# A linear-attention block with a gated feed-forward on one core: the query products regrouped around a burst of k^T v, and the gate and up weights loaded from the first query group on

## The chip, the cores and the metric

The kernel runs on one core of one Trainium2 chip. The metric is the device time of one execution in microseconds, the median of several runs. Of the kernel before there are three: 271.57, 271.64 and 271.98 us, median 271.64.

The core's engines run programs of their own and meet at semaphores: TensorE (PE in the profile, with its weight loads as PEld) multiplies matrices into PSUM, ScalarE (ACT) and VectorE (DVE) do elementwise work and read PSUM, GpSimd (POOL) does elementwise work on SBUF, and SyncE (SP) issues DMA transfers.

## What is computed

One sequence of S = 2048 rows with D = 640 columns. First a layer norm and linear attention with H = 32 heads of 20 columns, then a layer norm and a gated feed-forward of width F = 1536; each adds its input back.

```python
q, k, v = split_heads(layernorm(x) @ wqkv)
pq, pk = q @ w_phi[h], k @ w_phi[h]
phi_q = concat(softmax(pq), softmax(-pq)); phi_k = concat(softmax(pk), softmax(-pk))
kv = sum_s phi_k[s].T @ v[s];   z = sum_s phi_k[s]
o = (phi_q @ kv) / (phi_q @ z + 1e-6)
h = x + o @ wo
h2 = h + (gelu(layernorm(h) @ w_gate) * (layernorm(h) @ w_up)) @ w_down
```

## The kernel before

The rows are cut into 16 tiles of 128, four tiles make a block, and the 640 columns are cut into five chunks of 128. TensorE's and SyncE's order is written out by hand in the source, and within the kernel's main part that of the other engines too; each engine runs its instructions strictly in that order.

In the first part w_phi is folded into the weights of k and q, and a loop over the tiles (line 494) makes, for each tile, the key features (k_tile: ten products, two exponentials on ScalarE), the values (v_mm, v_ev) and the sums and factors that normalise the features (k_norm: VectorE sums, takes reciprocals, and GpSimd and VectorE multiply). kv_tile (line 368) adds a tile's phi_k^T v into the PSUM tile kvp with 32 small products a tile. It is called in bursts: tiles 0 to 3 at t = 9, 4 to 8 at t = 13, 9 to 12 at t = 15 (the third burst, table KVQ), and 13 to 15 after the loop (the last burst). Each burst needs the normalised features of its tiles.

The query features are made per block and chunk: product number 5 b + c is block b, chunk c. The table QG (line 52) groups them; a group of one or two such products, each five matmuls of 512 columns (one for each chunk of the inner dimension), has one PSUM tile of two banks and one SBUF tile Eq. q_mm(j) (line 387) issues the matmuls of group j, q_exp(j) (line 399) two exponentials on ScalarE over the whole group, one for each sign. The first four groups, (5, 6), (0, 1), (2, 3) and (4,), are made at t = 15 (table QT); the third burst stands behind the second group, (0, 1). The fifth group, (7, 8), follows the last burst, and its last matmul stands behind the first tile's attention (lines 831 to 835). Block 0 is chunks 0 to 4; block 1 is 5 to 9.

kv_mask (line 377) lets VectorE mask and transpose the finished kvp into KV; from then on attn_a (line 648) multiplies query features with KV, attn_b, attn_b2 and attn_b3 divide, the result o is transposed (for tile 0 by a DMA on SP's queue, for tile 1 on TensorE) and attn_c multiplies it with W_o. Behind that come the second layer norm, gate_up (line 758) and down (line 775), woven with the attention of later tiles.

The weights W_gate (tile Wg) and W_up (Wu) arrive by SP's queue. A GpSimd copy of one column from Eq into Wg (line 536) holds the first transfer of Wg back until group 2's second exponential, since the transfer writes what the copy wrote; two transfers of Wg's first four fifths follow at once (line 538). The rest of Wg and all of Wu are issued by load_up (line 551), which is called behind attn_b3(0), so that in SP's queue they stand behind the transpose of tile 0's o.

PSUM is handed out as four tiles of two banks each; a matmul that writes a tile waits until whoever read the tile earlier is done.

Of the kernel before, what the change touches and what calls it, by code (L numbers as in the profile page):

```python
# [11 lines left out]
ACTF = mybir.ActivationFunctionType  # L12
# [5 lines left out]
def kernel(  # L18
# [12 lines left out]
    nc = tc.nc  # L31
# [8 lines left out]
    NC = D // P  # L40
# [8 lines left out]
    LQ = (7, 8, 9, 9, 10)  # L49
    FQ = (10, 11, 12, 13, 14)  # L50

    QG = ((5, 6), (0, 1), (2, 3), (4,), (7, 8), (9, 10), (11, 12), (13, 14), (15,), (16,), (17,), (18,), (19,))
    QT = (15, 15, 15, 15)
    T3 = 3

# [32 lines left out]
    Wg = const.tile([P, NC, FF], BF16, name="Wg")  # L88
    Wu = const.tile([P, NC, FF], BF16, name="Wu")
# [5 lines left out]

    Eq = [const.tile([P, len(g), 2, 512], BF16, name=f"Eq{j}") for j, g in enumerate(QG)]
    ident = const.tile([P, P], BF16, name="ident")
# [5 lines left out]
    def eq(t, c, s):  # L103
        for E, g in zip(Eq, QG):
            if t // 4 * NC + c in g:
                return E[:, g.index(t // 4 * NC + c), s, t % 4 * P:(t % 4 + 1) * P]
# [4 lines left out]
    def gtile(name):  # L111
        return psG.tile([P, 2, 512], F32, name=name, tag="G")
# [46 lines left out]
    def transpose_to(dst, src, on_pe, on_dve=False):  # L159

        if on_pe:
            tp = psG.tile([P, 16, P], BF16, name="tp", tag="G")
            for c in range(NC):
                nc.tensor.transpose(tp[:, c, :], src[:, c * P:(c + 1) * P], ident)  # L164
            (nc.vector.tensor_copy if on_dve else nc.scalar.copy)(dst, tp[:, 0:NC, :])  # L165
        else:
            nc.sync.dma_start_transpose(dst, src)
# [32 lines left out]
    def load_T(WT, i, *ds):  # L200

        for d in ds:
            nc.sync.dma_start_transpose(WT[:, :, d * P:(d + 1) * P], A_wqkv[d * P:(d + 1) * P, i * D:(i + 1) * D])
# [3 lines left out]
    wg_v = B_w_gate.rearrange("(c p) n -> p c n", p=P)  # L207
    wu_v = B_w_up.rearrange("(c p) n -> p c n", p=P)
# [23 lines left out]
    def fold(WT, W2, quarters, ds=range(NC)):  # L232


        n, w = (2, QF) if quarters else (1, HD)
        runs = []
        for c in range(NC):
            lo, hi = H0[c] * Dh, (H0[c] + NH[c]) * Dh
            for r in range(2 * n):
                a, b = max(lo, r * w), min(hi, (r + 1) * w)  # L240
                if a < b:
                    runs.append((r // n, r, c, a, b))
        runs.sort()
        for d in ds:
            wa = gtile("wa")
            wr = wa.rearrange("p u (q x) -> p (u q) x", q=n)
            for i, (u, r, c, a, b) in enumerate(runs):
                nc.tensor.matmul(wr[:, r, a - r * w:b - r * w], lhsT=WT[:, c, d * P:(d + 1) * P],  # L248
                                 rhs=BD[:, c].rearrange("p a b -> p (a b)")[:, a - H0[c] * Dh:b - H0[c] * Dh],
                                 start=(i == 0 or runs[i - 1][0] != u),  # L250
                                 stop=(i + 1 == len(runs) or runs[i + 1][0] != u), skip_group_check=True)
            dst, src = W2[:, d, :].rearrange("p (u f) -> p u f", u=2), wr[:, :, 0:w]
            if quarters:
                dst = W2[:, d, :].rearrange("p (c r f) -> p r c f", c=NC, r=4)
                src = src.rearrange("p r (c f) -> p r c f", c=NC)
            if d in (QA if quarters else KA):
                nc.scalar.copy(dst, src)
            else:
                nc.vector.tensor_copy(dst, src)
# [15 lines left out]
    def ln_st(*tiles, act=True, between=None, log=False):  # L275
        for t, v in zip(tiles, ln_stats(p1, [x_sb[t // 4][:, t % 4, :] for t in tiles], "1", act, between, log)):
            lnp[t] = v

    def ln_ap(t, on_act=False, on_pe=False):
        ln = (ln_act if on_act else ln_dve)(p1, "1", *lnp[t])  # L280
        if on_pe:
            lnp[t] = ln
        else:
            transpose_to(LN1T[t // 4][:, :, t % 4 * P:(t % 4 + 1) * P], ln, False)
# [16 lines left out]
    def v_mm(t, us=(0, 1)):  # L301
        if 0 in us:
            pv[t] = gtile("pv")
        proj(pv[t], t, Wv, us)
# [10 lines left out]
    def v_ev(t):  # L315
        nc.scalar.activation(vS[t % NV][:, :, 1:VC].rearrange("p (u h) f -> p u h f", u=2),
                             pv[t][:, :, 0:HD].rearrange("p u (h f) -> p u h f", f=Dh), ACTF.Copy,
                             scale=lnp[t][2] if t in CT else 1.0)
# [12 lines left out]
    def k_tile(t):  # L331
        if t in pks:
            pk = pks[t]
            k_part(t, NC - 1)
        else:
            pk = gtile("pk")
            proj(pk, t, Wk2)
        Ek[t] = ev.tile([P, 2, D], BF16, name="E", bufs=10)
        for s in range(2):
            nc.scalar.activation(Ek[t][:, s, :].rearrange("p (u f) -> p u f", u=2), pk[:, :, 0:HD],  # L340
                                 ACTF.Exp, scale=((lnp[t][2], nrstd[t]) if t in CT else (1.0, -1.0))[s])
# [26 lines left out]
    def kv_tile(t):  # L368

        E = Ek[t].rearrange("p s (h f) -> p s h f", f=Dh)  # L370
        for i in range(QH):
            for r in range(4):
                h = r * QH + i
                nc.tensor.matmul(kvp[QUAD[r], :, i * Dh:(i + 1) * Dh], lhsT=vF[t % NV][:, h * VC:h * VC + 32],  # L374
                                 rhs=E[:, :, h, :], start=(i == t == 0), stop=(t == NT - 1), skip_group_check=True)
# [9 lines left out]
    pqs = {}  # L385

    def q_mm(j, part=(0, 1), kcs=range(NC)):

        if 0 in part and 0 in kcs:
            pqs[j] = gtile("pq")  # L390
        for i, bc in enumerate(QG[j]):
            if i not in part:
                continue
            b, c = divmod(bc, NC)
            for kc in kcs:
                nc.tensor.matmul(pqs[j][:, i, :], lhsT=Wq2[:, kc, c * P:(c + 1) * P], rhs=LN1T[b][:, kc, :],  # L396
                                 start=(kc == 0), stop=(kc == NC - 1))

    def q_exp(j, signs=(0, 1)):
        for s in signs:  # L400
            nc.scalar.activation(Eq[j][:, :, s, :], pqs[j][:, 0:len(QG[j])], ACTF.Exp, scale=(1.0, -1.0)[s])  # L401

    def st_act(t, i):

# [89 lines left out]
    for t in range(NT):  # L494
        if t == T3:
            kvp = gtile("kvp")[:, 0, 0:2 * QF].rearrange("p (s f) -> p s f", s=2)
        late = t in (1, 4)
        if 0 < t < NT - 6 and not late:
            ln_ap(t + 6, on_act=True)
        k_tile(t)  # L500
        if t == 0:
            ln_ap(6)
            nc.sync.dma_start(x_sb[3][:, 0:2, :], x_v[:, 12:14, :])
        if t in FQ:
            fold(WqT, Wq2, True, [i for i, f in enumerate(FQ) if f == t])
        for i in KVG.get(t, ()):
            kv_tile(i)
        for j in range(len(QT)):
            if t == QT[j]:
                q_mm(j)  # L510
                q_exp(j)
                for i in KVQ.get(j, ()):
                    kv_tile(i)
        if 0 < t < NT - 3:
            v_mm(t + 3)
        if late:
            ln_ap(t + 6, on_act=True)
        if t == 1:
            nc.sync.dma_start(x_sb[3][:, 2:4, :], x_v[:, 14:16, :])
        if 0 < t < NT - 3:  # L520
            v_ev(t + 3)
        for i in ST.get(t, ()):
            ln_st(i, i + 1)
        k_norm(t)
        load_T(WqT, 0, *[i for i, f in enumerate(LQ) if f == t])
        if t == 10:
            transpose_to(LN1T[0][:, :, P:2 * P], ln_a(1), False)
        if t == 13:
            ln_ap(0, on_act=True)
        if t == 8:  # L530
            for z in KT:
                nc.gpsimd.memset(z, 0.0)
        if t == 13:
            nc.sync.dma_start(Wo, wo_v)
    q = len(QT)
    nc.gpsimd.tensor_copy(Wg[:, 0, 0:1], Eq[q - 2][:, 0, 1, 0:1])
    for a, b in ((0, 2), (2, 4)):
        nc.sync.dma_start(Wg[:, a:b], wg_v[:, a:b])
    for t in range(13, NT):
        kv_tile(t)  # L540
    kv_mask()
# [5 lines left out]
    p2r = ctx.enter_context(tc.tile_pool(name="p2r", bufs=1, side="right", reuse_waits="tile"))  # L547
    Wd = p2r.tile([P, NF, D], BF16, name="Wd")
    wd_v = B_w_down.rearrange("(c p) n -> p c n", p=P)

    def load_up():

        nc.sync.dma_start(Wg[:, 4:NC], wg_v[:, 4:NC])
        nc.sync.dma_start(Wu, wu_v)

    def load_down(*fs):

# [271 lines left out]


    q_mm(q, (0,))
    q_mm(q, (1,), (0, 1, 2, 3))
    attn_a(0, 1)
    q_mm(q, (1,), (4,))
    q_exp(q)
    q_mm(q + 1)
    attn_b(0, True)
    attn_b2(0, True)
    attn_b3(0)
    load_up()  # L840
    attn_a(1, 0)
    q_exp(q + 1, (0,))
    q_mm(q + 2)
# [93 lines left out]
```

## Time and profile before

| | before |
|---|---|
| median of 3 runs | 271.64 us |
| profiled execution | 272.4 us |
| its span | 270.7 us |
| TensorE busy | 265.7 us |
| VectorE, ScalarE, GpSimd busy | 174.9, 138.9, 101.2 us |
| query products (L396) | 100, 379 ns each |
| query exponentials (L401) | 26, 831 ns each in the mean |
| W_gate's first two transfers issued | 67.80 us |
| W_up issued, to landing | 76.36 us, 8.9 us |

The profile is one execution on the chip. Its page gives busy time by engine, the chain of work that ended last, and groups of instructions. In a timeline a row has start, length, engine, source line, operation, what it writes and reads, how many of them follow one another, and in brackets the engine's idle time before it and what ended it. Matmuls overlap, so a row's length is from the first one's start to the last one's modelled end. SPq rows are issues of transfers, not the transfers.

### The profile page before, as it was taken

To read this page: it belongs to the slowest core of one execution; us is meant where nothing else is said; L and a number is where in the kernel's file an instruction comes from. 1 tells how busy PE (TensorE), PEld (TensorE's weight loads), DVE (VectorE), ACT (ScalarE), POOL (GpSimd) and SP (SyncE) were. 2 spreads that over 40 slices of the span, in tenths; PEclk is the share of its full clock that TensorE was granted. 3 is DMA by queue.
4 is the path that set the end of the run, shared out by engine and by line. 5 is a ranking of instruction groups with operands and counts; after the bars stand their busy time and mean duration, and the time that the engine had idled before them with its cause. 6 is when DMAs were issued, how large, how long until landed. Compare 5 with 4: busy or idle time off the path is not lost.

```text
span 270.7 us, 7046 instructions
## 1 busy us (share of the span) xinstructions
PE 265.7 (98%) x2867; PEld 171.3 (63%) x2867; DVE 174.9 (65%) x347; ACT 138.9 (51%) x249; POOL 101.2 (37%) x238
## 2 busy tenths in 40 slices
PE   7999999999999999999999999999999999999995
PEld 6777777755455877788755455775555476444574
DVE  5889999996877767876466783568673332333322
ACT  5789998876789675245541356421544300322100
POOL 5548988796002335376211564014661100000000
PEclk9999999999999999999999999999999999999999
DMA  6998257250678432442201222102222101000011
GB/s 187 225 199 169 54 99 110 38 150 2 234 246 244 155 101 56 41 104 51 52 24 51 48 50 51 48 3 75 77 44 52 24 24 51 24 0 0 4 48 48
DMA packets 45264, 22.10 MB, mean 82 GB/s; under 512 B 37808, under 2 KB 43184, under 8 KB 45232
## 3 DMA queue, kind: packets, MB, share of 16 engines
q1 hardware_dynamic: 44576, 21.64, 32.6%
q8 instruction: 22, 0.36, 0.6%
q10 hardware_dynamic: 656, 0.03, 0.2%
q14 instruction: 10, 0.08, 0.1%
HBM read 10.18 MB, written 2.62 MB: 47 GB/s over the span
## 4 chain that ended last, share of the span: by engine, by line
PE 96%; DMA 2%; SPq 0%; issue 0%; DVE 0%
PE gu L767 39%; PE pd L789 19%; PE pq L396 8%; PE pk L296 8%; PE po L707 8%; PE pv L296 7%; PE kvp L374 2%; PE pv L312 2%; DMA Wv<-in_A_wqkv_dram 2%; PE ab L618 1%; PE wa L248 1%; PE ab L585 1%; PE tp L164 0%; SPq L193 0%; SPq L190 0%
## 5 line engine op out<-in xcount | busy, mean ns | idle before, releaser
L770 ACT ACTIVATE g<-gu 128x512 bf16<-128x512 f32 (+1 forms) x60 | 30.4, 510 | 73.8 <-PE gu L767 72.9
L773 DVE TENSOR_TENSOR GT<-gu,g 128x512 bf16<-128x512 f32 (+1 forms) x60 | 34.4, 580 | 46.7 <-PE gu L767 38.8
L767 PE MATMUL gu<-LN2T,Wg 128*128 128x512 bf16 (+1 forms) x300 | 61.8, 337 | 0.0
L767 PE MATMUL gu<-LN2T,Wu 128*128 128x512 bf16 (+1 forms) x300 | 61.7, 336 | 0.0
L789 PE MATMUL pd<-Wd,GT 128*128 128x320 bf16 (+4 forms) x396 | 53.9, 295 | 0.0
L789 PEld LDWEIGHTS <-GT 128*128 128x128 bf16 x396 | 37.6, 98 | 14.5 <-DVE GT L773 0.2
L767 PEld LDWEIGHTS <-Wu 128*128 128x128 bf16 x300 | 29.4, 98 | 22.6
L767 PEld LDWEIGHTS <-Wg 128*128 128x128 bf16 x300 | 29.0, 98 | 21.2
L296 PEld LDWEIGHTS <-LN1T 128*128 128x128 bf16 x290 | 27.9, 98 | 10.5
L355 POOL TENSOR_TENSOR E<-E,rs 128x640 bf16<-128x640 bf16 x25 | 31.6, 1299 | 4.4 <-DVE rs L351 4.1
L791 DVE TENSOR_TENSOR y<-pd,x_sb 128x320 bf16<-128x320 f32 (+4 forms) x33 | 15.8, 480 | 24.2 <-PE pd L789 24.2
L707 PE MATMUL po<-Wo,oT 128*128 128x320 bf16 x160 | 24.5, 299 | 0.0
L296 PE MATMUL pk<-Wk,LN1T 128*128 128x320 bf16 x160 | 24.4, 299 | 0.0
L396 PE MATMUL pq<-LN1T,Wq 128*128 128x512 bf16 x100 | 22.9, 379 | 0.0
L347 DVE TENSOR_REDUCE sk<-E 128x64 f32<-128x1280 bf16 x16 | 22.9, 1430 | 0.0
L401 ACT ACTIVATE Eq<-pq 128x1024 bf16<-128x1024 f32 (+1 forms) x26 | 19.9, 831 | 3.5 <-PE pq L396 3.3
L340 ACT ACTIVATE E<-pk 128x640 bf16<-128x640 f32 x28 | 18.7, 746 | 3.0 <-PE pk L296 3.0
L707 PEld LDWEIGHTS <-oT 128*128 128x128 bf16 x160 | 15.6, 98 | 7.3 <-ACT oT L165 0.2
L296 PE MATMUL pv<-Wv,LN1T 128*128 128x320 bf16 x130 | 19.8, 299 | 0.0
L151 ACT ACTIVATE ln<-x_sb,v,rstd 128x640 bf16<-128x640 bf16 x14 | 12.9, 920 | 13.4 <-POOL v L746 13.2
L396 PEld LDWEIGHTS <-Wq 128*128 128x128 bf16 x100 | 9.4, 98 | 10.3
L682 DVE TENSOR_TENSOR tt<-AB,w 128x1280 bf16<-128x1280 f32 x10 | 15.1, 1506 | 0.4 <-POOL w L675 0.3
(120 smaller groups left out, 290.6 us busy)
## 6 DMA issues: line engine op xcount, KB each, us to landing
out_dram<-y SPq DMA_DIRECT2D x15, 160.0 KB, 1.8
x_sb<-in_A_x_dram SPq DMA_DIRECT2D x6, 320.0 KB, 4.0
Wu<-in_B_w_up_dram SPq DMA_DIRECT2D x1, 1920.0 KB, 8.9
Wg<-in_B_w_gate_dram SPq DMA_DIRECT2D x2, 768.0 KB, 5.8
Wd<-in_B_w_down_dram SPq DMA_DIRECT2D x1, 1440.0 KB
Wo<-in_A_wo_dram SPq DMA_DIRECT2D x1, 800.0 KB, 5.2
x_sb<-in_A_x_dram SPq DMA_DIRECT2D x4, 160.0 KB, 3.3
Wv<-in_A_wqkv_dram SPq DMA_DIRECT2D x2, 320.0 KB, 4.2
```

The lines of the kernel that those rows point to most:

```text
L296: nc.tensor.matmul(ps[:, u, 0:HD], lhsT=lnT(t, c), rhs=W[:, c, u * HD:(u + 1) * HD], start=(c == 0), stop=(c == NC - 1))
L340: nc.scalar.activation(Ek[t][:, s, :].rearrange("p (u f) -> p u f", u=2), pk[:, :, 0:HD], ACTF.Exp, scale=((lnp[t][2], nrstd[t]) if t in C ...
L347: nc.vector.reduce_sum(sk, Ek[t].rearrange("p s (h f) -> p (s h) f", f=Dh), axis=AX.X)
L355: eng.tensor_tensor(e, e, rs[:, s * H:(s + 1) * H, None].to_broadcast([P, H, Dh]), ALU.mult)
L396: nc.tensor.matmul(pqs[j][:, i, :], lhsT=Wq2[:, kc, c * P:(c + 1) * P], rhs=LN1T[b][:, kc, :], start=(kc == 0), stop=(kc == NC - 1))
L401: nc.scalar.activation(Eq[j][:, :, s, :], pqs[j][:, 0:len(QG[j])], ACTF.Exp, scale=(1.0, -1.0)[s])
L707: nc.tensor.matmul(pos[u], lhsT=st[t][:, c, :], rhs=Wo[:, c, u * HD:(u + 1) * HD], start=(c == 0), stop=(c == NC - 1))
L767: nc.tensor.matmul(gu[i][:, 0:n], lhsT=W[:, c, f * P:(f + 1) * P], rhs=LN2T[b][:, c, a0:a1], start=(c == 0), stop=(c == NC - 1))
L770: nc.scalar.activation(g[:, 0:n], gu[0][:, 0:n], ACTF.Gelu_apprx_tanh)
L773: nc.vector.tensor_tensor(st[b, "g", f][:, a0:a1], gu[1][:, 0:n], g[:, 0:n], ALU.mult)
L789: nc.tensor.matmul(pd[:, 0:f1 - f0], lhsT=st[b, "g", f][:, tl * P:(tl + 1) * P], rhs=Wd[:, f, f0:f1], start=(f == 0), stop=(f == NF - 1), ...
L791: nc.vector.tensor_tensor(y[:, f0:f1], pd[:, 0:f1 - f0], x_sb[b][:, tl, f0:f1], ALU.add)
```

## The change

The group table becomes (5, 6), (7,), (0, 1), (2, 3), (4, 8), and so on. At t = 15 the order is now (5, 6), (7,), the third burst, (0, 1), (2, 3), then as before the last burst. The fifth group is (4, 8): chunk 4 of block 0 and chunk 8 of block 1. Its first product is followed by its own two exponentials (q_exp gets a part), then comes the second product, the attention of tile 0, and the exponentials of the second product. The GpSimd copy waits for the first group's exponentials and stands inside the loop, ahead of k_norm(15). All of Wg and Wu is issued in one go, behind the copy and ahead of the transpose of o.

```diff
-    QG = ((5, 6), (0, 1), (2, 3), (4,), (7, 8), (9, 10), ...
+    QG = ((5, 6), (7,), (0, 1), (2, 3), (4, 8), (9, 10), ...
...
-    def q_exp(j, signs=(0, 1)):
+    def q_exp(j, signs=(0, 1), part=None):
+        i = slice(0, len(QG[j])) if part is None else slice(part, part + 1)
         for s in signs:
-            nc.scalar.activation(Eq[j][:, :, s, :], pqs[j][:, 0:len(QG[j])], ACTF.Exp, scale=(1.0, -1.0)[s])
+            nc.scalar.activation(Eq[j][:, i, s, :], pqs[j][:, i], ACTF.Exp, scale=(1.0, -1.0)[s])
...
                 q_mm(j)
                 q_exp(j)
+                if j == 0:
+                    nc.gpsimd.tensor_copy(Wg[:, 0, 0:1], Eq[j][:, 0, 1, 0:1])
                 for i in KVQ.get(j, ()):
                     kv_tile(i)
...
     q = len(QT)
-    nc.gpsimd.tensor_copy(Wg[:, 0, 0:1], Eq[q - 2][:, 0, 1, 0:1])
-    for a, b in ((0, 2), (2, 4)):
+    for a, b in ((0, 2), (2, 4), (4, NC)):
         nc.sync.dma_start(Wg[:, a:b], wg_v[:, a:b])
+    nc.sync.dma_start(Wu, wu_v)
...
-    def load_up():
-        nc.sync.dma_start(Wg[:, 4:NC], wg_v[:, 4:NC])
-        nc.sync.dma_start(Wu, wu_v)
...
     q_mm(q, (0,))
-    q_mm(q, (1,), (0, 1, 2, 3))
+    q_exp(q, part=0)
+    q_mm(q, (1,))
     attn_a(0, 1)
-    q_mm(q, (1,), (4,))
-    q_exp(q)
+    q_exp(q, part=1)
     q_mm(q + 1)
     attn_b(0, True)
     attn_b2(0, True)
     attn_b3(0)
-    load_up()
     attn_a(1, 0)
```

More of the change, by code (lines that the diff above doesn't have):

```diff
@@ L50 @@
     FQ = (10, 11, 12, 13, 14)
-    QG = ((5, 6), (0, 1), (2, 3), (4,), (7, 8), (9, 10), (11, 12), (13, 14), (15,), (16,), (17,), (18,), (19,))
+    QG = ((5, 6), (7,), (0, 1), (2, 3), (4, 8), (9, 10), (11, 12), (13, 14), (15,), (16,), (17,), (18,), (19,))
     QT = (15, 15, 15, 15)
```

## The prediction

> **What bounds the kernel now.** I read the page first, then the list of waits between 56 and 72 us, then each engine's timeline there, and last the DMA view of narrow windows.
>
> ```profile
> span 270.7 us, 7046 instructions
> PE 265.7 (98%) x2867; PEld 171.3 (63%) x2867; DVE 174.9 (65%) x347; ACT 138.9 (51%) x249; POOL 101.2 (37%) x238
> PE 96%; DMA 2%; SPq 0%; issue 0%; DVE 0%
> ```
>
> TensorE is busy for 98% and carries 96% of the chain that ended last. So time is lost only where TensorE stands, and a transfer or an exponential that comes sooner gains nothing unless TensorE stood for it. The timeline of TensorE, over all that the change moves:
>
> ```profile
> 57.04 4.48 PE L396 MATMUL pq<-LN1T,Wq 128*128 128x512 bf16 x20
> 61.45 1.04 PE L374 MATMUL kvp<-E,vS 128*32 128x40 bf16 x109
> 62.98 0.30 PE L374 MATMUL kvp<-E,vS 128*32 128x40 bf16 x19 [0.48 <-issue]
> 63.21 3.41 PE L396 MATMUL pq<-LN1T,Wq 128*128 128x512 bf16 x15
> 66.56 0.94 PE L374 MATMUL kvp<-E,vS 128*32 128x40 bf16 x96
> 67.42 2.12 PE L396 MATMUL pq<-LN1T,Wq 128*128 128x512 bf16 x9
> 69.47 0.47 PE L585 MATMUL ab<-KV,Eq 32*128 32x44 bf16 x40
> ```
>
> There is one hole: the third burst of k^T v (tiles 9 to 12) stops behind its 109th product for 0.48 us. "issue" means that no semaphore ended it, and a data wait could only stand at a tile's first product (the 97th is tile 12's). I take it for a wait for code. The DMA view has an instruction queue (q8), 22 packets in the whole run. With 5,734 loads and products on TensorE (2867 of each), that is one packet for each 260. Window 56 to 60.6 us, then 60.6 to 61.8, then 61.8 to 64:
>
> ```profile
> DMA packets 1311, 0.97 MB, mean 211 GB/s; under 512 B 682, under 2 KB 1311, under 8 KB 1311
> Wo<-in_A_wo_dram SPq DMA_DIRECT2D x1, 800.0 KB, 5.2
> ...
> DMA packets 18, 0.03 MB, mean 25 GB/s; under 512 B 6, under 2 KB 17, under 8 KB 17
> q8 instruction: 1, 0.02, 5.4%
> ...
> DMA packets 0, 0.00 MB, mean 0 GB/s; under 512 B 0, under 2 KB 0, under 8 KB 0
> ```
>
> The code block moved right behind Wo's 0.8 MB, landed before 61.8, and TensorE went on at 62.98. Nothing else moved meanwhile. So the hole's end hangs on a transfer, a fixed time; its start hangs on how soon TensorE uses up the code it has.
>
> **The change part by part.** Sums are made against the profiled execution: 272.4 us, span 270.7. The median of the timed runs is 271.64, 0.76 below; I add the differences to the median.
>
> *1. Group (7,) ahead of the third burst, in place of (0, 1).* The lengths of one product of each kind:
>
> ```profile
> L396 PE MATMUL pq<-LN1T,Wq 128*128 128x512 bf16 x100 | 22.9, 379 | 0.0
> L374 PE MATMUL kvp<-E,vS x512: 179/187/194, 38.8 to 67.3; 128*32 128x40 bf16 x171
> ```
>
> No product is added. Twenty products take 4.48, one takes 0.38, so one follows the other after (4.48 - 0.38) / 19 = 0.216 us. Five fewer stand ahead of the burst: it starts 5 x 0.216 = 1.08 us sooner, at 60.37. The program ahead of it is shorter by those five loads and products and one wait, 11 instructions; the code block's end, at the same instruction number, now lies behind the 114th product instead of the 109th. At 0.008 us each (1.04 less one product's 0.19, over 108) that is 0.04. TensorE runs dry 1.04 sooner. Wo and the code packet don't know of the change, since up to the first group all is as before. So the hole ends at 62.98 again and is 1.04 longer. The five products come after it, with nobody waiting meanwhile: **+1.04 us**. Bounds: +1.04 if the block's arrival ends the hole; 0 if the hole has a length of its own; -0.68 if it is gone (start to start: 62.98 less 61.45 + 1.04 - 0.19).
>
> Tile 12's factors are no new wait: VectorE's and GpSimd's work for it is done by then.
>
> ```profile
> 54.45 10.45 POOL L355 TENSOR_TENSOR E<-E,rs 128x640 bf16<-128x640 bf16 x8 [1.63 <-DVE rs L351]
> 63.04 1.86 POOL L355 TENSOR_TENSOR E<-E,rs 128x640 bf16<-128x640 bf16 x1
> 67.58 0.19 POOL L536 COPY Wg<-Eq 128x1 bf16<-128x1 bf16 x1 [2.68 <-ACT Eq L401]
> ```
>
> These eight are tiles 11 (two), 12 (two), 13 (two), 14 and 15; at 1.3 each tile 12 is done at 59.7, and tile 12 is wanted at 61.1.
>
> *2. Group (4, 8), with an exponential between its halves.* This is the dear part. q_exp(q, part=0) now stands between q_mm(q, (0,)) and q_mm(q, (1,)), and both halves lie in one PSUM tile. The built program of the changed kernel shows what comes of it: the sixth product of the group waits for ScalarE, and the count that it waits for is reached by the second of part 0's two exponentials.
>
> ```
> L396 Ldweights Wq2_102
> L396 Matmult pq_1643<-LN1T_101,Wq2_102 128x512 [waits Activation_49]
> L396 Ldweights Wq2_102
> L396 Matmult pq_1643<-LN1T_101,Wq2_102 128x512
> ```
>
> In the old order all ten came before any exponential, so before has no such wait. Its price, with T the end of the last burst, from these rows (ScalarE; then the load that follows an ACT copy):
>
> ```profile
> 59.40 1.94 ACT L401 ACTIVATE Eq<-pq 128x1024 bf16<-128x1024 f32 x2 [0.70 <-PE pq L396]
> 65.58 2.92 ACT L401 ACTIVATE Eq<-pq 128x1024 bf16<-128x1024 f32 x4 [2.08 <-PE pq L396]
> 86.00 1.09 ACT L401 ACTIVATE Eq<-pq 128x512 bf16<-128x512 f32 x2 [0.32 <-PE pq L396]
> ...
> 78.67 0.69 ACT L165 COPY oT<-tp 128x640 bf16<-128x640 bf16 x1 [0.71 <-PE tp L164]
> 79.42 0.10 PEld L707 LDWEIGHTS <-oT 128*128 128x128 bf16 x1 [0.17 <-ACT oT L165]
> ```
>
> The fifth product ends at T + 4 x 0.216 + 0.38 = T + 1.24. An exponential follows 0.04 behind (the first group's tenth product ends at 57.04 + 9 x 0.216 + 0.38 = 59.36, its exponential starts at 59.40): T + 1.28. Two of 512 columns take 1.09: T + 2.37. TensorE goes on 0.06 behind (79.36 to 79.42): T + 2.43, where it would have gone on at T + 1.08. **+1.35 us**. Lower bound 1.15, the two exponentials and the hand-over alone, if the products' ends are modelled late. Upper bound 1.6, if ScalarE is late: the exponentials of (2, 3) start 0.04 behind their products (66.62 in before, T - 0.80), take 1.94, and end at T + 1.2, only 0.1 before they would be in the way. Queued behind the waiting product on TensorE is everything: the second half, the attention of tile 0 and all after it.
>
> The old order hid VectorE's masking and transposing of k^T v behind nine products:
>
> ```profile
> 67.58 0.45 DVE L381 TENSOR_SCALAR KT<-kvp,sc,bi 128x160 bf16<-128x160 f32 x1 [2.00 <-PE kvp L374]
> 69.00 0.58 DVE L383 STREAM_TRANSPOSE KV<-KT 128x384 bf16<-128x384 bf16 x1
> ```
>
> It ends at T + 2.16; the attention now starts at T + 3.5. No second wait, and no gain either, since TensorE went straight on at 69.47 in before. ScalarE runs 28 exponentials for 26, three narrow pairs (1.09) and three wide for one and four (1.94), 0.24 us more, off the path.
>
> *3. GpSimd's copy and the weights.* The copy now waits for the first group's exponentials (61.34) and stands ahead of tile 15's product on GpSimd, behind tile 14's, which ends at 63.04. It delays tile 15 by 0.19, to 65.1; TensorE wants that in the last third of the last burst, after 67. Nothing; without that cover 0.19. On SP's queue W_gate's last fifth and W_up move ahead of the transpose of o.
>
> ```profile
> 67.80 0.89 SPq L538 DMA_DIRECT2D Wg<-in_B_w_gate_dram  x2
> 74.48 1.21 SPq L167 DMA_TRANSPOSE oT<-o  x1
> 76.36 0.42 SPq L554 DMA_DIRECT2D Wu<-in_B_w_up_dram  x1
> 70.00:71.00 1.00, 1.00 (x6) 0.43 (x5) 0.88 (x1) 0.94 (x2) 0.00 (x0) 1.00 1.04 418
> Wu<-in_B_w_up_dram SPq DMA_DIRECT2D x1, 1920.0 KB, 8.9
> 86.86 0.71 PE L767 MATMUL gu<-LN2T,Wu 128*128 128x256 bf16 x5
> ```
>
> These rows are SP's timeline, the second 70 to 71 (last figure GB/s), the page's transfer of W_up and its first use. W_gate and W_up have 1920 KB each, 3.93 MB; issued from 63.3, at 418 GB/s, they are through at about 74. The transpose of o, moved to about 76.9 by the two waits, finds the queue free: nothing. Were the waits not there, it would come at 74.5 right behind W_up, at most 0.3 late. W_up landed at 85.3 in before and was first used at 86.86 with no wait of TensorE, so being sooner gains nothing.
>
> *Sum:* 1.04 + 1.35 = **+2.4 us**, profiled 274.8, **median 274.0**.
>
> The Trainium skill ("Runtime: NRT & Kernel Launch", Instruction fetch mechanics) says that code comes in 16 KiB blocks of 256 instructions over a queue of its own, the next one while the current one runs, so that crossing a block is mostly hidden. The trace agrees on the size (0.36 MB in 22) and not on the hiding, if I read the hole rightly; by the page the hole would not move, and the sum would be +1.35 (rival A).
>
> **Rivals.**
> - **A, the hole has its own length:** it comes where it comes and lasts 0.68. For it: only one hole is there to judge by. Against: the last burst runs 96 products without one, and the code packet lies just ahead. +1.35: 273.0.
> - **B, the hole closes**, since the code is there in time in an unprofiled run: 1.35 - 0.68 = +0.7, 272.3.
> - **C, the early weights hold up a code block.** The next packet moved between 63 and 65.1 us, in an empty queue; in the changed kernel the weights start near 64.3:
>
> ```profile
> q8 instruction: 1, 0.02, 2.8%
> ...
> q8 instruction: 1, 0.02, 5.5%
> ```
>
>   The second row is the window 72.5 to 73.6: the packet after that came only as W_gate's transfer ran out. A packet that starts behind the weights comes near 73, while TensorE wants it one block (some 260 instructions) after the hole, at the end of the last burst, 66.56 + 0.8 + 1.04 = 68.4. From 73 and the 1.2 us that lay between landing and going on in before: some +6 on top, 280. It decides whether the packet starts before 64.3; I expect it at 63, 1 us sooner than before, as the burst is.
> - **D, faster:** the burst has its code in time and the second half doesn't stand, because ScalarE is done with part 0 when the fifth product's successor is due. Then -0.68: 271.0. It needs the pair of exponentials over by T + 1.08, before their products end at T + 1.24; that decides against it.
> - That the early loads do nothing, with nobody waiting for them, is part of the forecast.
>
> **How the numbers follow.** Forecast 0.60 (273.7 to 274.4), A 0.21 (273.0), B 0.06 (272.3), C 0.08 (280), D 0.05 (271.0). The range 272.7 to 274.7 holds forecast and A with the bounds of the wait (1.15 to 1.6) and leaves out B, C, D, 0.19. About 0.2% (0.54 us) is what a measurement can tell from no change. Slower 0.95, same 0.02, faster 0.03 (D, near the limit, gives to both).
>
> **What would show it.** Right: the third burst starts near 60.4 and is broken behind its 114th product until about 63.0; the fifth product of group (4, 8) is followed by 1.35 us without TensorE, ended by ScalarE; W_gate issued near 63.3; no wait of TensorE for oT or gu. Wrong: a hole that moves with the burst (A), none (B), one of several us near 68 (C), or no hole inside the group (D).

## The result and the profile after

The kernel after takes 274.14 us (median of 8 runs, 272.85 to 274.79); the kernel before, run beside it, 271.87 (8 runs, 271.57 to 272.51). The ratio is 1.0074, its 95% interval 1.0052 to 1.0096: slower by 2.0 us, with 1.4 to 2.6 by the interval. The forecast was 274.0, within 272.7 to 274.7. The profiled execution is the fastest of its eight, 272.85 us; that matters below. In the experiments, one execution of e1 (276.73 us), two of e5 (277.01 and 277.23) and four of e4 (276.35 to 276.64, and the profiled one of 395.03) ran at a granted TensorE clock of 0.994 or less (0.998 to 1.0 in all the others): the medians given include them, but nothing is read from their times.

First the page of after: span, engines, the shares of the chain, the group of the query products. Against before, where that group's idle time was 0.0, one thing is new.

```profile
span 271.1 us, 7049 instructions
PE 265.7 (98%) x2867; PEld 171.1 (63%) x2867; DVE 173.8 (64%) x347; ACT 139.0 (51%) x251; POOL 101.6 (37%) x238
PE 96%; DMA 1%; SPq 0%; ACT 0%; issue 0%; DVE 0%
L396 PE MATMUL pq<-LN1T,Wq 128*128 128x512 bf16 x100 | 23.1, 379 | 1.2 <-ACT Eq L402 1.2
```

ScalarE now stands in the chain, and the query products wait 1.2 us for Eq. Next TensorE's timeline of after, over the stretch that the prediction showed of before:

```profile
56.86 3.40 PE L396 MATMUL pq<-LN1T,Wq 128*128 128x512 bf16 x15
60.19 1.20 PE L374 MATMUL kvp<-E,vS 128*32 128x40 bf16 x128
61.33 4.49 PE L396 MATMUL pq<-LN1T,Wq 128*128 128x512 bf16 x20
65.75 0.94 PE L374 MATMUL kvp<-E,vS 128*32 128x40 bf16 x96
66.61 1.25 PE L396 MATMUL pq<-LN1T,Wq 128*128 128x512 bf16 x5
69.04 1.24 PE L396 MATMUL pq<-LN1T,Wq 128*128 128x512 bf16 x5 [1.17 <-ACT Eq L402]
70.21 0.47 PE L583 MATMUL ab<-KV,Eq 32*128 32x44 bf16 x40
...
73.28 4.92 PE L396 MATMUL pq<-LN1T,Wq 128*128 128x512 bf16 x22
78.04 0.84 PE L705 MATMUL po<-Wo,oT 128*128 128x320 bf16 x5
```

Three readings. The sixth product of group (4, 8) starts at 69.04; five products behind 66.61 it was due at 66.61 + 5 x 0.216 = 67.69: 1.35 us lost. The third burst is one row of 128 products: this execution has no hole at all. And the first product with oT follows its neighbour without a bracket (78.04 - 73.28 = 4.76, the plain length of 22 products). So this execution differs from the profiled one of before by +1.35 and by -0.68, the hole that isn't there; 0.18 more is an earlier start of the first q group (56.86 for 57.04). That makes +0.49, and the span grew by 271.1 - 270.7 = 0.4.

ScalarE's, GpSimd's and SP's rows of after, a fence for each:

```profile
65.85 3.14 ACT L402 ACTIVATE Eq<-pq 128x1024 bf16<-128x1024 f32 x4 [0.22 <-PE pq L396]
```

```profile
62.85 0.78 POOL L514 COPY Wg<-Eq 128x1 bf16<-128x1 bf16 x1
63.59 1.86 POOL L355 TENSOR_TENSOR E<-E,rs 128x640 bf16<-128x640 bf16 x1
```

```profile
63.66 1.40 SPq L540 DMA_DIRECT2D Wg<-in_B_w_gate_dram  x3
65.11 0.59 SPq L541 DMA_DIRECT2D Wu<-in_B_w_up_dram  x1
75.22 1.20 SPq L167 DMA_TRANSPOSE oT<-o  x1
```

The four exponentials end at 65.85 + 3.14 = 68.99, and TensorE goes on 0.05 behind. The weights are issued at 63.66 and the transpose of o at 75.22. Two rows of the windows of after (last figure GB/s) and one DMA issue show how near that was:

```profile
74.00:75.00 1.00, 1.00 (x6) 0.42 (x5) 0.97 (x2) 1.00 (x3) 0.00 (x0) 1.00 0.94 366
75.00:76.00 1.00, 1.00 (x6) 0.48 (x5) 0.90 (x5) 1.00 (x2) 0.00 (x0) 1.00 0.08 31
```

```profile
oT<-o SPq DMA_TRANSPOSE x1, 2.5
```

The weights' traffic falls to 31 GB/s at 75.0, the transpose is issued 0.2 behind that and lands after 2.5 us, for 2.4 in before. Last, the DMA view of after from 58.0 to 59.2 us, in 40 slices of 0.03:

```profile
GB/s 128 589 128 171 43 43 43 128 128 43 128 128 128 256 43 213 128 213 341 299 341 299 299 341 256 384 341 384 341 341 427 341 469 341 341 384 341 469 384 384
q1 hardware_dynamic: 234, 0.30, 79.8%
q8 instruction: 1, 0.02, 4.9%
```

The code packet's bytes are the peak in the second slice, so it starts at 58.03; 4.9% of 16 engines over 1.2 us is 0.94, so it lands at 59.0. Here it came **before** most of W_o's data; in before it started at about 60.6, **behind** them, and landed at 61.7. All packet times below are read so.

**Theory** after this: the wait for the exponentials is there in every execution. The hole is a wait for code and hangs on whether the code packet comes before or behind W_o's data, which changes from one execution to the next; TensorE goes on some 1.3 us after its landing. **Rivals**: the hole belongs to its place in the program and has a fixed length; it is an accident of one execution of before and plays no part; the early weights cost something of their own.

### The profile page after: what moved, and what is told of

Same layout as the page of the kernel before. It is cut to its first block, busy times and chain, and to the rows that moved or that the text cites. A ratio compares the mean times of both kernels' runs of the same rounds, so it can differ in the third digit from the quotient of the medians.

```text
span 271.1 us, 7049 instructions
## 1 busy us (share of the span) xinstructions
PE 265.7 (98%) x2867; PEld 171.1 (63%) x2867; DVE 173.8 (64%) x347; ACT 139.0 (51%) x251; POOL 101.6 (37%) x238
## 4 chain that ended last, share of the span: by engine, by line
PE 96%; DMA 1%; SPq 0%; ACT 0%; issue 0%; DVE 0%
PE gu L765 38%; PE pd L787 19%; PE pq L396 8%; PE pk L296 8%; PE po L705 8%; PE pv L296 7%; PE kvp L374 2%; PE pv L312 2%; DMA Wv<-in_A_wqkv_dram 1%; PE ab L616 1%; PE wa L248 1%; PE ab L583 1%; PE tp L164 0%; ACT Eq L402 0%; SPq L193 0%; SPq L190 0%
## 5 line engine op out<-in xcount | busy, mean ns | idle before, releaser
L765 PE MATMUL gu<-LN2T,Wg 128*128 128x512 bf16 (+1 forms) x300 | 61.8, 337 | 0.0
L765 PE MATMUL gu<-LN2T,Wu 128*128 128x512 bf16 (+1 forms) x300 | 61.7, 336 | 0.0
L402 ACT ACTIVATE Eq<-pq 128x512 bf16<-128x512 f32 (+1 forms) x28 | 20.1, 784 | 3.0 <-PE pq L396 2.8
```

The costliest lines, as they stand in the source:

```text
L402: nc.scalar.activation(Eq[j][:, i, s, :], pqs[j][:, i], ACTF.Exp, scale=(1.0, -1.0)[s])
L765: nc.tensor.matmul(gu[i][:, 0:n], lhsT=W[:, c, f * P:(f + 1) * P], rhs=LN2T[b][:, c, a0:a1], start=(c == 0), stop=(c == NC - 1))
```

## The experiments

Of eleven kernels, each stood beside runs of the kernel before, whose medians were 271.94 to 272.04. "Due" means the start that a product would have had at the plain pace (0.216 us from one query product to the next, 4.76 for 22 of them).

**e1: the changed kernel again**, with no edit.

> The changed kernel once more. Theory: two added costs, a wait of 1.35 us for part 0's exponentials in every execution, and a hole in the third burst that is there only when the code block comes behind W_o's data (0 or up to 1.7 us). So the executions spread from about 272.8 to 274.8, and the profile shows a hole of 0 to 1.7 us behind the 114th product, ended at the code block's landing. Rival (the hole has nothing to do with the code block): times within 0.3 us of each other, and a hole of a fixed length or none.

274.6 us (6 runs, 273.07 to 276.73), ratio 1.0093 [1.0057, 1.0129]. TensorE and, for 59.2 to 60.4 us in slices of 0.03, the DMA view:

```profile
60.31 1.09 PE L374 MATMUL kvp<-E,vS 128*32 128x40 bf16 x114
61.59 0.27 PE L374 MATMUL kvp<-E,vS 128*32 128x40 bf16 x14 [0.19 <-issue]
...
69.51 1.24 PE L396 MATMUL pq<-LN1T,Wq 128*128 128x512 bf16 x5 [1.18 <-ACT Eq L402]
```

```profile
GB/s 384 384 427 887 384 384 341 469 256 384 384 341 427 256 512 213 469 427 299 427 299 427 299 384 427 299 512 213 427 427 299 427 256 512 213 427 341 256 256 256
q8 instruction: 1, 0.02, 4.9%
```

Same program, another execution, and the hole is back, behind the 114th product as forecast. The packet starts at 59.3 (the peak of 887), in the midst of W_o's data, lands at 60.25, and TensorE goes on at 61.59, 1.34 later. Product 115 was due at 60.31 + 1.09 - 0.19 = 61.21, so 0.38 is lost. The wait for the exponentials is the same to 0.01.

**e2: W_o's load out of the way, behind W_gate's first part.**

```diff
-        if t == 13:
-            nc.sync.dma_start(Wo, wo_v)
...
         nc.sync.dma_start(Wg[:, a:b], wg_v[:, a:b])
+        if a == 0:
+            nc.sync.dma_start(Wo, wo_v)
```

> The changed kernel, with W_o's transfer issued behind W_gate's first part (about 64 us) in place of about 56. Theory: the code block for the end of the third burst finds an empty queue, the hole is gone in every execution: 272.8, all within 0.4 us, and only the wait for the exponentials is left in the trace. Rival (the hole doesn't come from W_o): median and spread stay, 274.1 and 2 us.

275.31 us (6 runs, 274.7 to 276.01), ratio 1.0121 [1.0101, 1.0141]. Slower, where the theory had it faster (272.8): a miss in the total.

```profile
60.64 1.20 PE L374 MATMUL kvp<-E,vS 128*32 128x40 bf16 x128
...
73.73 4.92 PE L396 MATMUL pq<-LN1T,Wq 128*128 128x512 bf16 x22
80.45 0.85 PE L705 MATMUL po<-Wo,oT 128*128 128x320 bf16 x5 [1.80 <-DMA oT<-o]
```

The hole is gone in its profile, but the loads now run longer than the transpose of o can wait. W_o's product was due at 73.73 + 4.76 = 78.49 and starts 1.96 late, for oT, which landed 4.7 us after its issue for 2.5 in after. So the third part of the change, the early weights, has a price as soon as the queue behind them is longer; in after it is hidden.

**e3: the second half of a group gets a PSUM tile of its own.** The sixth product then writes a tile that no exponential reads.

```diff
+        if part == (1,) and len(QG[j]) > 1:
+            pq1[j] = gtile("pq")
...
-                nc.tensor.matmul(pqs[j][:, i, :], lhsT=Wq2[:, kc, c * P:(c + 1) * P], ...
+                nc.tensor.matmul(pq1.get(j, pqs[j])[:, i, :], lhsT=Wq2[:, kc, c * P:(c + 1) * P], ...
...
-            nc.scalar.activation(Eq[j][:, i, s, :], pqs[j][:, i], ACTF.Exp, ...
+            nc.scalar.activation(Eq[j][:, i, s, :], (pq1[j] if part == 1 else pqs[j])[:, i], ACTF.Exp, ...
```

> The changed kernel, with a PSUM tile of its own for the second product of group (4, 8). Theory: the wait of 1.34 us goes, since it is for the tile alone; nothing takes its place, as the attention's inputs are ready by then: 1.3 less than the changed kernel beside it, so about 272.8 with the hole's spread (271.5 to 273.4). Rival (the attention then waits for k^T v or part 0): under 0.4 us less.

273.4 us (8 runs, 272.49 to 274.15), ratio 1.0055 [1.0037, 1.0072].

```profile
66.62 2.33 PE L398 MATMUL pq<-LN1T,Wq 128*128 128x512 bf16 x10
...
71.96 4.92 PE L398 MATMUL pq<-LN1T,Wq 128*128 128x512 bf16 x22
77.64 0.85 PE L707 MATMUL po<-Wo,oT 128*128 128x320 bf16 x5 [0.76 <-DMA oT<-o]
```

```profile
73.89 1.20 SPq L167 DMA_TRANSPOSE oT<-o  x1
```

```profile
oT<-o SPq DMA_TRANSPOSE x1, 3.7
```

The ten products run through in 2.33, so the wait came from the shared tile. But in this execution only a part of it is won: everything behind is 1.3 us sooner, the transpose of o is issued at 73.89, while the weights still run, lands after 3.7 us, and W_o's product, due at 76.72, starts 0.92 late. One wait had hidden another. Between the profiled executions of after and e3, both without a hole, 0.36 us is won (272.85 and 272.49); between the medians of e1 (without its 276.73) and e3 it is 1.1. A hole delays the transpose too and would shorten the wait for it, which fits, but no profile has both.

**e4: both edits of e2 and e3 together.**

> Both edits, W_o late and a PSUM tile of its own. Theory: neither hole nor wait is left; 271.5, all within 0.4 us, which is before without its hole, and 0.3 to 0.4 under the median of before. Rival (the early weights or the moved burst cost something of their own): 272 or more.

276.38 us, ratio 1.0144 [1.0119, 1.0169]: a miss, where the theory had 271.5. It stands above e2 only by the executions named at the start; the other two took 274.99 and 275.33, within e2's range. The profiled execution is one of those named, so no row tells where the time went. After e2 and e3 it can be argued, not shown: the long queue of loads of e2 meets the earlier transpose of e3, and the split tile then wins nothing.

**e5: the regrouping alone**, with all loads as in before.

```diff
-                if j == 0:
-                    nc.gpsimd.tensor_copy(Wg[:, 0, 0:1], Eq[j][:, 0, 1, 0:1])
...
-    for a, b in ((0, 2), (2, 4), (4, NC)):
+    nc.gpsimd.tensor_copy(Wg[:, 0, 0:1], Eq[q - 2][:, 0, 1, 0:1])
+    for a, b in ((0, 2), (2, 4)):
         nc.sync.dma_start(Wg[:, a:b], wg_v[:, a:b])
-    nc.sync.dma_start(Wu, wu_v)
...
     attn_b3(0)
+    nc.sync.dma_start(Wg[:, 4:NC], wg_v[:, 4:NC])
+    nc.sync.dma_start(Wu, wu_v)
     attn_a(1, 0)
```

> The changed kernel's groups and order, with the loads of W_gate and W_up as in before. Theory: the early loads cost and gain nothing in the changed kernel, whose transpose of o comes just after them; wait and hole remain: median 274.1 to 274.6, spread 2 us as in the changed kernel. Rival (the early loads make the slow executions, by the transpose of o behind them): 272.9 to 273.2, with a spread under 0.6 us.

273.75 us (11 runs, 273.12 to 277.23), ratio 1.0072 [1.0044, 1.0099]. The median lies between the theory (274.1 to 274.6) and the rival (272.9 to 273.2). Without the two executions named at the start it is 273.65, 1.6 above before: most of the loss of the change comes with the regrouping, and whether all of it does isn't shown. In its profile the burst is whole and the wait is there:

```profile
61.01 1.20 PE L374 MATMUL kvp<-E,vS 128*32 128x40 bf16 x128
...
69.86 1.24 PE L396 MATMUL pq<-LN1T,Wq 128*128 128x512 bf16 x5 [1.17 <-ACT Eq L402]
```

**e6: the early weights alone**, in the kernel before.

```diff
+                if j == 0:
+                    nc.gpsimd.tensor_copy(Wg[:, 0, 0:1], Eq[j][:, 0, 1, 0:1])
...
-    for a, b in ((0, 2), (2, 4)):
+    for a, b in ((0, 2), (2, 4), (4, NC)):
         nc.sync.dma_start(Wg[:, a:b], wg_v[:, a:b])
+    nc.sync.dma_start(Wu, wu_v)
...
-    load_up()
```

> Before's groups and order, with the early loads alone. Theory: without the wait for exponentials the transpose of o is issued at about 74.5 and comes behind W_up, lands near 77.6, and TensorE stands for it 0.2 us (with the hole of before) to 0.9 us (without): median 272.5, lowest 272.3. Rival (hidden, as the prediction had it): 271.9, as before.

272.98 us (5 runs, 272.78 to 273.36), ratio 1.0037 [1.0025, 1.0049]: 1.0 us slower than before, and 0.5 more than expected.

```profile
72.30 4.91 PE L396 MATMUL pq<-LN1T,Wq 128*128 128x512 bf16 x21
78.22 0.85 PE L709 MATMUL po<-Wo,oT 128*128 128x320 bf16 x5 [1.02 <-DMA oT<-o]
```

```profile
oT<-o SPq DMA_TRANSPOSE x1, 4.2
```

Due at 72.30 + 4.76 = 77.06, W_o's product starts 1.16 late, for oT. The early loads are not free; the changed kernel's other wait pays for them.

**e7: W_o's load two tiles sooner in the changed kernel**, so that its data are through when the packet is asked for.

```diff
-        if t == 13:
+        if t == 11:
             nc.sync.dma_start(Wo, wo_v)
```

> The changed kernel with W_o issued sooner, at about 53 us behind the transpose of tile 1, so that it is through before the code block is wanted. Theory: the hole is gone and the wait of 1.34 us alone is left: 272.8, all within 0.5 us. Rival (the slow executions have another cause): median 274.1 or more, spread 2 us.

273.24 us (5 runs, 273.06 to 273.57), ratio 1.0047 [1.0035, 1.0059]. The burst is whole, the wait for the exponentials stays, and the executions lie within 0.5 us instead of 1.9. The median is 0.4 above the theory's 272.8; the profiled execution is 0.72 above after's, as much as its burst starts later (60.91 for 60.19); e9 asks whether that comes from W_o's place. The rows:

```profile
60.91 1.20 PE L374 MATMUL kvp<-E,vS 128*32 128x40 bf16 x128
...
69.77 1.24 PE L396 MATMUL pq<-LN1T,Wq 128*128 128x512 bf16 x5 [1.17 <-ACT Eq L402]
```

**e8: the changed groups with e3's tile, e7's W_o and the loads of W_gate and W_up as in before**: everything that was found to cost is taken out, the order of the bursts stays.

> The changed groups with a PSUM tile of its own for product (8,), W_o sooner, and the loads of W_gate and W_up as in before. Theory: no wait for exponentials, no hole and no wait for the transpose: 271.5, all within 0.4 us, a little under the median of before (271.9). Rival (W_o sooner holds up something else): over 272.

272.07 us (12 runs, 271.79 to 272.68), ratio 0.9999 [0.9989, 1.0009]: no difference from before.

```profile
60.73 1.20 PE L374 MATMUL kvp<-E,vS 128*32 128x40 bf16 x128
...
67.15 2.33 PE L398 MATMUL pq<-LN1T,Wq 128*128 128x512 bf16 x9
...
72.48 4.92 PE L398 MATMUL pq<-LN1T,Wq 128*128 128x512 bf16 x21
77.24 0.84 PE L705 MATMUL po<-Wo,oT 128*128 128x320 bf16 x5
```

None of the three waits is left, and with them the loss is gone. There is no gain behind it either; 271.5 was expected. (Some records of products are missing, x9 for 10; the times show that they ran.)

**e9: W_o two tiles sooner in the kernel before**, the edit of e7.

> The kernel before with one edit: W_o's load is issued two tiles sooner (at t = 11), so that its data are through before the code block of the third burst is asked for. Theory (the hole in the third burst is a code packet held behind W_o's data): no hole in the burst, so up to 0.68 us less, 271.3 to 271.8, and a spread over the executions below 0.5 us instead of 1. Rival 1 (the hole is a property of the instruction's place): 0.48 us idle behind the 109th product as in before, the time that of before within 0.2. Rival 2 (loading W_o so early costs something of its own in the first part, about 0.4 us, as the burst's start of 60.7 to 60.9 in two earlier runs may mean): no hole, but the first q group starts later than 57.04 by some 0.4, time 271.9 to 272.3.

271.9 us (12 runs, 271.62 to 273.06), ratio 1.0 [0.9988, 1.0013]. The profile (271.66 us) has what the theory wanted, the median and the spread of 1.4 us have not:

```profile
57.02 4.48 PE L396 MATMUL pq<-LN1T,Wq 128*128 128x512 bf16 x20
61.43 1.20 PE L374 MATMUL kvp<-E,vS 128*32 128x40 bf16 x128
```

The first group starts at 57.02 (57.04 in before), so W_o's early load costs nothing in this profile; the later starts in other profiles (57.58 in e7, and 57.67 in e5, where W_o isn't early) look like a scatter of executions. The burst is whole: the code packet starts at 58.2, for 60.6 in before, with TensorE's rows ahead of it the same to 0.02. This profile's time is 0.74 below before's profile, near the hole's 0.68. That the median doesn't move points to a median execution of before with **no** hole to speak of; its profiled one had it.

**e10: the suspected cost made larger**: W_up's 1.92 MB right behind W_o's 0.8 MB in the changed kernel.

```diff
             nc.sync.dma_start(Wo, wo_v)
+            nc.sync.dma_start(Wu, wu_v)
...
-    nc.sync.dma_start(Wu, wu_v)
```

> The changed kernel with W_up's 1.92 MB issued right behind W_o at t = 13 instead of behind W_gate: the suspected cost is made larger, as 2.7 MB instead of 0.8 MB now lie around the time at which the third burst's code block is asked for (57.7 to 60.3 us). Theory (packet behind bulk data): where the packet is asked for behind the issue of W_up, it lands near 57.5 + 2.7 MB at 400 GB/s = 64, TensorE runs dry near 61.4 behind the 114th product and goes on 1.3 us behind the landing: a hole of 1 to 4 us and 275 to 278 us. Where the packet is asked for ahead of it, no hole and 273 to 274. In return W_gate alone is through before the transpose of tile 0's o, which then lands in 2.4 us. Rival (the hole is a fixed cost of the instruction's place, or the packet goes ahead of bulk data): hole of 0 to 0.5 us as before, 273.5 to 274.5.

274.65 us (4 runs, 274.01 to 274.78), ratio 1.0087 [1.0064, 1.0109]. TensorE, and the DMA view from 60.6 to 61.8 us:

```profile
60.27 1.08 PE L374 MATMUL kvp<-E,vS 128*32 128x40 bf16 x114
63.05 0.27 PE L374 MATMUL kvp<-E,vS 128*32 128x40 bf16 x14 [1.69 <-issue]
```

```profile
GB/s 102 350 614 1058 102 307 717 410 102 307 717 410 102 410 614 410 102 512 614 307 102 512 614 307 102 614 614 205 307 410 614 205 307 512 512 307 307 512 614 102
q8 instruction: 1, 0.02, 5.0%
```

Product 115 was due at 60.27 + 1.08 - 0.19 = 61.16: a hole of 1.89 us, the largest of all, against the rival of a fixed length. But the packet started at 60.7, not near 64 as the theory said: W_up's data run all around it and hold it back no further. In this one profile it comes behind what W_o has queued, not behind all that is queued later. The time is below the theory's 275 and about that of e1.

**e11: the changed groups with e3's tile and all loads as in before**, W_o too: e8 without its early W_o.

> The changed groups alone, with a PSUM tile of its own for the second product of the fifth group and the loads as in the kernel before (W_o too): neither the wait for the exponentials nor the early weights are left, only the earlier third burst. Theory (the earlier burst costs only where the code packet comes behind W_o): 272.0 to 273.2, 0 to 1 us over before, the executions spread over 1 to 2 us, depending on the packet. Rival (the prediction's first part in full, a hole that always ends at the same time): before + 1.04, 273.0, with little spread. Rival (the regrouping itself is free and no hole matters): that of the same kernel with W_o early, 272.07, spread below 0.9.

272.76 us (12 runs, 271.94 to 274.5), ratio 1.0031 [1.0012, 1.005]. The profiled execution took 273.87; TensorE and the DMA view from 60.7 to 61.9 us:

```profile
60.61 1.08 PE L374 MATMUL kvp<-E,vS 128*32 128x40 bf16 x114
63.31 0.27 PE L374 MATMUL kvp<-E,vS 128*32 128x40 bf16 x14 [1.62 <-issue]
```

```profile
GB/s 0 546 0 0 0 0 0 0 0 0 0 0 0 0 0 0 0 0 0 0 0 0 0 0 0 0 0 0 0 0 0 0 0 0 0 0 0 0 0 0
q8 instruction: 1, 0.02, 5.6%
```

Here the packet is alone: it starts at 60.73 when W_o's data are through, lands at 61.8, and TensorE, which wanted product 115 at 61.50, goes on at 63.31: 1.81 lost. The other executions go down to 271.94, where no such hole can be: without it that would be 270.1, and no execution of before is under 271.49. The median is 0.82 above before and 0.69 above e8, from which this kernel differs only in W_o's place. This is the price of the earlier burst by itself, on the median.

## Why the prediction was right, and where it wasn't

**Group (4, 8), +1.35: right.** Measured 1.35 in after (1.17 of it as idle time), the same in e1, e5 and e7 to 0.01, and gone in e3 when the PSUM tile was split. The working held row by row: the exponentials end 0.05 before TensorE goes on, and no second wait follows in the attention.

**The third burst, +1.04: right in its mechanism, wrong as a fixed amount.** The place was exact: behind the 114th product in e1, e10 and e11. Where the packet comes behind W_o, so was the size: 0.68 + 1.04 = 1.72 predicted, 1.81 and 1.89 measured. The step that failed is "Wo and the code packet don't know of the change ... the hole ends at 62.98 again". In the changed order, with W_o where it was, the packet starts anywhere from 58.0 to 60.7, and the hole is 0 (after; e3 and e5 too, with starts at 58.6 and 58.2), 0.38 (e1) or 1.8 to 1.9 (e11, e10). On the median it costs 0.82 (e11 against before), or 0.69 (e11 against e8).

The prediction had a sign of this in its numbers and passed it over. The profiled execution was 0.76 above the median, and the hole was 0.68, which points to a median run without a hole. e9 bears that out, and so does e6: with before's order of products and W_o in its old place its profile has a whole burst (128 products in 1.20 us from 61.59) and a packet that starts at 59.0. No profile of the kernel before itself shows it. On this reading, adding the difference to the median came out by luck: the median went from no hole to some 0.8, not from 0.68 to 1.72. The rule of the Trainium skill ("Runtime: NRT & Kernel Launch", Instruction fetch mechanics), that crossing a code block is mostly hidden, holds in after's profile, where the packet landed at 59.0, and not where it landed at 61.7 to 61.8.

**The weights and GpSimd's copy, 0: right for this kernel, for a reason that was only half seen.** No wait for oT or gu came, as forecast. But "at most 0.3 late" without the other waits was wrong: 0.92 (e3), 1.16 (e6). The weights were through, but for a rest, at 75.0 instead of about 74. And a transpose that is issued while they run doesn't come 0.3 later; it lands after 3.7 to 4.7 us instead of 2.4. In after's profile the transpose was issued 0.2 us behind the time at which the weights' traffic fell off.

**The sum, +2.4:** measured 2.0 by the ratio (1.4 to 2.6), 2.27 by the medians. The parts measured apart: 0.82 for the earlier burst (e11) and 1.17 for the wait with the early weights (e7 less e8), together 2.0. Part by part it closes, with less for the burst.

**The rivals.** A (a hole of fixed length) falls with 0, 0.38 and 1.8 in one order of the program. B (no hole) is what after's profiled execution shows, the fastest of its eight. C (the early weights hold up a code block) isn't seen: no hole near 68 in after. Its condition didn't arise, since the packet in question started at 61.9, ahead of the weights' issue at 63.66. The next packet, at 69.85, did start in the midst of their data (the window from 69.0 to 70.2 us ran at 421 GB/s), and no wait of TensorE followed. D fell, as the pair of exponentials does end behind the time at which the sixth product was due.

**Open.** What decides in an execution whether the packet comes before or behind W_o's data wasn't found, and the hole is known only in the profiled executions. The narrow spread of e7 has only five runs behind it; e9, whose profile has no hole, spreads over 1.4, and the first query group starts anywhere from 56.86 (after, e3) to 57.67 (e5), so other things scatter too. None of the kernels beat before.

## What to carry to other kernels

A hole that no semaphore ends, right behind a large load, can be a thing of single executions: hold the profiled execution's distance from the median against the hole before taking it as a constant. A finer order can help only if the framework's unit of dependence, here the PSUM tile, is made finer with it (here it then cost nothing, and gained nothing either). And when loads are moved ahead, look at the next small transfer that someone waits for: it can be late by more than the loads' tail, and another wait may hide it until that wait is mended.

## What the hardware showed beyond that

- Where TensorE stood for its code, it went on 1.3 to 1.5 us after the packet had landed (before 61.7 to 62.98, e1 60.25 to 61.59, e10 61.7 to 63.05, e11 61.8 to 63.31).
- The code packet started only at 60.6 to 60.8, as W_o's 0.8 MB ran out, in before, e10 and e11, and no later when 1.92 MB more were queued right behind those (e10, one profile); in e9, with W_o out of the way, it started at 58.2.
- A DMA transpose issued while bulk loads ran landed after 3.7 us in e3, 4.2 in e6 and 4.7 in e2; the traffic stayed at 350 GB/s and more for another 1.1, 1.5 and 1.8 us behind its issue (windows of half a microsecond). Against that stand 2.4 to 2.5 us where the loads were through but for a rest (before, after).
